# Projecting q and k of the last four head groups beside sliding-window attention, with x loaded a second time

## The chip, the cores and the metric

The kernel runs on one core of one Trainium2 chip. The metric is the device time of the whole launch in microseconds (us); lower is better. The engines named below are PE (matrix multiply; PEld is its weight load), DVE (vector), ACT (activation functions), POOL (general purpose) and SP, whose queue issues every DMA of this kernel.

## The reference

The reference computes windowed attention and an MLP from the same `x` and mixes the two with a gate for each row. Cut to what matters:

```python
B, S, D = 1, 2048, 512          # F = 1792, H = 32 heads of 16, window W = 256
qkv = x @ wqkv                   # split into q, k, v, each [H, S, 16]
scores = q @ k.T * 16 ** -0.5    # kept where 0 <= row - column < 256
a = softmax(scores) @ v          # heads joined again, then a = a @ wo
b = gelu(x @ w1 + b1) @ w2 + b2
g = sigmoid((x * gate_w).sum(-1, keepdims=True))
out = g * a + (1 - g) * b
```

## The kernel before

**Precision.** Every large product is made of three matmuls (`mm3`, L109 to L111): each operand is held as a rounded high part and a low rest, and high by high, high by low and low by high are added in PSUM. One such triple of 512 columns is the unit of dense work; the kernel's own planner books `MM3` = 681 ns for it.

**Tiles.** S is cut into four tiles `t` of 512 rows (`T`), each tile into four blocks of 128. D has four chunks `c`. `wqkv` gives, for each tile, eight pieces for q and k (`qk_j`, four of each) and four for v (`v_b`). A piece is four triples. The 32 heads are eight head groups of four. Pieces j = 0, 1 of q and j = 4, 5 of k hold head groups 0 to 3, and j = 2, 3, 6, 7 hold groups 4 to 7.

**Dense work.** `dense()` is a generator that yields after each triple. It goes through `qkv(t)` for four tiles, then through eight turns of the MLP (`TURNS`: half of F, tile), each of them a part u (7 tiles of `x @ w1`, with the GELU as four ACT and three DVE instructions behind each) and a part y (the product with `w2`), and at last through `final(t)`, the product with `wo` (tile name `a`).

**Attention.** It runs through 128 units `u` of 128 keys (8 groups by 16 blocks). In each there are four scores for the row maximum (`sm`, L522, reduced on DVE at L527, 12 units ahead), four scores transposed (`st`, L567, then exp on ACT at L589) and, behind every fourth unit, a run of small matmuls with v (`pv`, L611). Loads for it go four units and more ahead: `kd`, `qd`, `ks`, `qs`, `vbuf`.

**Order.** All five engines run in the order in which the program was written out. A planner interleaves the two streams by a clock `now` of its own: `fill(ns)` takes that much dense work from the generator, `after(ns, f)` writes f out so many ns later, `need(key)` writes out what is due until key is there. Dense work alone fills the first `START` = 105 us of the planner's clock. From there each attention unit is followed by `STEP0` = 2750 ns (before u = 0) or `STEP` = 2330 ns of dense work, spread over the unit's four scores: behind each pair of them, or behind each single one while an MLP u part is running. With these numbers the MLP's last turn ends when the attention does.

**q and k.** A piece is moved out of PSUM by ACT (high, L323) and DVE (low, L326) into a buffer of tag `h` (7 buffers) and stored to DRAM by two DMAs of 512 and 256 KB (`SQ`, `SK`); the attention loads are made from there. Weights come in as `raw` tiles, are split by ACT (L179) and by DVE or POOL (L183) into tag `w` (14 buffers); the list `later` holds those of the MLP and of `wo`. After `LAND` = 7500 ns from a load the planner writes out the ACT copy, which waits for the landing and holds up what stands behind it on ACT.

**x.** The transposed, split x of tile t is a buffer of 4 chunks by 512 KB. It is stored to DRAM (`XT`) and loaded again for each MLP turn (`mx`, tag `xt`, one buffer).

Of the kernel before, what the change touches and what calls it, by code (L numbers as in the profile page):

```python
# [18 lines left out]
T = 512  # L19
# [13 lines left out]
def gated_mix(ctx: ExitStack, tc: tile.TileContext, x, wqkv, wo, w1, b1, w2, b2, gate_w, out):  # L33
# [74 lines left out]
    def mm3(p, lh, ll, rh, rl, first, last):  # L108
        nc.tensor.matmul(p, lh, rh, start=first, stop=False)  # L109
        nc.tensor.matmul(p, lh, rl, start=False, stop=False)  # L110
        nc.tensor.matmul(p, ll, rh, start=False, stop=last)  # L111
# [19 lines left out]
    def need(*keys):  # L131
        for key in keys:
            while key not in done:
                step_todo()
# [154 lines left out]
    def gate_z(t, b):  # L289
# [2 lines left out]
        nb = t * NB + b  # L292
        nc.vector.tensor_tensor_reduce(junk, xr, gwb, 1.0, 0.0, ALU.mult, ALU.add, z[:, nb:nb + 1])

    def qkv_qk(t, j):

        xt = xts[t]
        w = wt["qk", j]
        p = ps.tile([128, T], F32, tag="d", bufs=2, name=f"qk{t}_{j}")
        for c in range(NC):  # L300
            mm3(p, w[:, 0, c], w[:, 1, c], xt[:, c, 0], xt[:, c, 1], c == 0, c == NC - 1)
            yield MM3
        qk_out(t, j, p)

# [59 lines left out]
    def warm(n):  # L364

        p = ps.tile([128, T], F32, tag="d", bufs=2, name=f"warm{now[0]}")
        for _ in range(n):
            nc.tensor.matmul(p[:, 0:320], idle[:, 0:128], idle, start=True, stop=True)
            tick(134)

    def qkv(t):
        last = t == NT - 1
        qk = [("qk", j) for i in range(NC) for j in (i, i + NC)]
        vs = [("v", b) for b in range(NB)]
        pieces = qk[:4] + vs + qk[4:] if last else qk + vs
        if t == 0:
            keys = qk + [("v", c) for c in range(NC)]
            load_xr(0, (0, 1))
            load_raw(keys[0], True)
            load_xr(0, (2, 3))  # L380
            for key in keys[1:]:
# [12 lines left out]
            split_now(keys[1], lambda o, i: nc.scalar.activation(o, i, AF.Copy), nc.vector)  # L394
            qkv_x(0, 3)
            parts = [(0, 0), (0, 1), (1, 0)]
            yield qk_half(p[1], j1, 0, parts)
            split(keys[2], nc.gpsimd)
            yield qk_half(p[0], j0, 1, parts)
            qk_out(0, j0, p[0])  # L400
            yield qk_half(p[1], j1, 1, parts)
            qk_out(0, j1, p[1])
        need(*[("x", t, b) for b in range(NB)])
        for n, (kind, j) in enumerate(pieces):
            if not last and XAT <= n < XAT + NC:
                nc.sync.dma_start(XT[t][n - XAT], f32(xts[t][:, n - XAT]))
            if kind == "qk":
                need(("w", (kind, j)))
            else:
                need(*[("w", ("v", c)) for c in range(NC)])  # L410
            if t == 0 and n == 10:
                nc.sync.dma_start(b1c, b1.rearrange("(f p) -> p f", p=128))
            if t == 0 and n < 2:
                pass
            elif kind == "qk":
                yield from qkv_qk(t, j)
            else:
                yield from qkv_v(t, j)
            if t == 1 and n % 3 == 2:
                clear_k(n // 3)  # L420
# [4 lines left out]
            if t == 2 and n in (8, 9):  # L425
                load_ks(0, n - 8)
            if t == 0:
                for i in ([3], [4], [5], [6], [7], [8], [9, 10], [11])[n] if n < 8 else []:
# [11 lines left out]
            xat = (5, 7, 8, 9) if t == 0 else (4, 6, 8, 10)  # L440
            if not last and n in xat:
                qkv_x(t + 1, xat.index(n))
            if not last and n == xat[-1] + 1:
                gate(t + 1)


    vts, Ms, pts = {}, {}, {}

# [224 lines left out]

    w1k = w1.rearrange("(c p) f -> p c f", p=128)

    def load_x(t, name):
        xt = sb.tile([128, NC, 2, T], F32R, tag="xt", bufs=1, name=f"{name}{t}")

        def part(c):
            nc.sync.dma_start(f32(xt[:, c]), XT[t][c])  # L680
            if c == NC - 1:
                done.add(name)
        for c in range(NC):
            after(MXAT * c, part, c)
        xts[t] = xt

    def load_o(t, cs=range(NC)):
# [82 lines left out]
    def mlp(n):  # L770
# [9 lines left out]
        for i in range(HF):  # L780
# [266 lines left out]
```

## Time and profile before

| | |
|---|---|
| timed runs | 749.82, 750.41, 750.96 us; median 750.41 |
| span of the profiled execution | 747.5 us |
| instructions in it | 17960 |
| PE busy | 732.3 us (98%) |
| DVE, ACT, POOL busy | 519.5, 421.8, 372.5 us |
| granted PE clock | 1.000 over the whole span |
| bytes moved by DMA | 172.12 MB, mean 230 GB/s |

The span reaches from the first to the last instruction of one profiled execution. That execution's time as a launch isn't listed by itself; the timed runs lie 2.3 to 3.5 us above the span. A matmul's end is modelled: one of 512 columns reads as 0.39 us long while the next starts 0.23 us after it, so the first 0.16 us of any wait of PE don't show as idle. In the profile's windows each stretch gives busy time and instruction counts for each engine, then the granted clock, the busy share of the DMA engines and the rate.

### The profile page before, as it was taken

To read this page: it belongs to the slowest core of one execution; us is meant where nothing else is said; L and a number is where in the kernel's file an instruction comes from. 1 tells how busy PE (TensorE), PEld (TensorE's weight loads), DVE (VectorE), ACT (ScalarE), POOL (GpSimd) and SP (SyncE) were. 2 spreads that over 40 slices of the span, in tenths; PEclk is the share of its full clock that TensorE was granted. 3 is DMA by queue.
4 is the path that set the end of the run, shared out by engine and by line. 5 is a ranking of instruction groups with operands and counts; after the bars stand their busy time and mean duration, and the time that the engine had idled before them with its cause. 6 is when DMAs were issued, how large, how long until landed. Compare 5 with 4: busy or idle time off the path is not lost.

```text
span 747.5 us, 17960 instructions
## 1 busy us (share of the span) xinstructions
PE 732.3 (98%) x6129; PEld 604.7 (81%) x6129; DVE 519.5 (69%) x1567; ACT 421.8 (56%) x972; POOL 372.5 (50%) x846
## 2 busy tenths in 40 slices
PE   8999999998999999999999999999999999999998
PEld 7888888876788888888887877888888888867786
DVE  4632425799768867886898689768867986784552
ACT  4434532358437835764695478437745853794550
POOL 4200000339756865876587668747765875630000
PEclk9999999999999999999999999999999999999999
DMA  9979898898995687799566889996799789558673
GB/s 318 336 243 408 288 391 282 254 311 194 263 258 132 173 238 205 178 220 265 155 169 156 237 209 232 257 231 154 179 262 238 185 204 287 138 179 230 205 235 113
DMA packets 179259, 172.12 MB, mean 230 GB/s; under 512 B 56672, under 2 KB 122976, under 8 KB 179168
## 3 DMA queue, kind: packets, MB, share of 16 engines
q1 hardware_dynamic: 179168, 170.97, 82.0%
q8 instruction: 49, 0.80, 0.5%
q14 instruction: 42, 0.34, 0.2%
HBM read 108.53 MB, written 62.39 MB: 229 GB/s over the span
## 4 chain that ended last, share of the span: by engine, by line
PE 85%; DVE 4%; DMA 3%; ACT 3%; issue 3%; POOL 1%; SPq 0%; DVEq 0%; ACTq 0%; POOLq 0%
PE sm L522 9%; PE st L567 8%; PE pv_sm L611 7%; PE y L109 7%; PE y L110 6%; PE y L111 6%; PE u L109 5%; PE u L110 5%; PE u L111 5%; PE qk L109 4%; PE qk L111 4%; PE qk L110 4%; PE a L109 2%; PE v L109 2%; PE v L111 2%
## 5 line engine op out<-in xcount | busy, mean ns | idle before, releaser
L527 DVE CUSTOM_DVE_ANT_0 jm<-sm,mask 128x320 bf16<-128x320 f32 (+4 forms) x512 | 237.9, 465 | 95.4 <-PE sm L522 61.0
L583 POOL TENSOR_SCALAR_AFFINE_SELECT pt<-pt 64x256 f32<-64x256 f32 (+1 forms) x538 | 227.6, 443 | 109.4 <-ACT pt L589 99.1
L589 ACT ACTIVATE pt<-st 128x320 f32<-128x320 f32 (+4 forms) x512 | 199.6, 424 | 139.0 <-PE st L567 135.4
L522 PE MATMUL sm<-kd,qd 96*128 96x320 f32 (+4 forms) x512 | 153.9, 312 | 6.9 <-DVE M L527 6.1
L567 PE MATMUL st<-qs,ks 128*128 128x320 f32 (+4 forms) x512 | 154.0, 309 | 1.9 <-ACT pt L589 1.9
L549 POOL CAST qs<-tt 4x256 fp32r<-4x256 f32 x256 | 124.2, 485 | 53.2 <-DVE tt L542 42.6
L522 PEld LDWEIGHTS sm<-kd,qd 96*128 96x128 f32 x512 | 96.4, 188 | 33.6 <-DVE M L527 14.2
L567 PEld LDWEIGHTS st<-qs,ks 128*128 128x128 f32 x512 | 97.1, 190 | 18.9 <-ACT pt L589 3.3
L109 PE MATMUL y<-w,h 128*128 128x512 f32 x224 | 88.6, 395 | 0.0
L110 PE MATMUL y<-w,h 128*128 128x512 f32 x224 | 87.9, 392 | 0.0
L111 PE MATMUL y<-w,h 128*128 128x512 f32 x224 | 87.9, 392 | 0.0
L109 PE MATMUL u<-mx,w 128*128 128x512 f32 x196 | 80.0, 408 | 0.0
L110 PE MATMUL u<-mx,w 128*128 128x512 f32 x196 | 77.3, 395 | 0.0
L111 PE MATMUL u<-mx,w 128*128 128x512 f32 x196 | 77.0, 393 | 0.0
L611 PE MATMUL pv_sm<-pt,vbuf 64*32 64x320 f32 (+4 forms) x1408 | 73.6, 346 | 0.2
L611 PE MATMUL pv_st<-pt,vbuf 64*32 64x320 f32 (+4 forms) x1408 | 73.3, 346 | 0.0
L611 PEld LDWEIGHTS pv_sm<-pt,vbuf 64*32 64x32 f32 x1408 | 50.2, 106 | 20.1 <-issue 2.4
L326 DVE TENSOR_TENSOR qke<-qk,qke 128x512 fp32r<-128x512 f32 x32 | 22.0, 688 | 45.9 <-ACT qke L323 38.5
L323 ACT ACTIVATE qke<-qk 128x512 fp32r<-128x512 f32 x32 | 19.1, 597 | 55.4 <-PE qk L111 32.9
L111 PEld LDWEIGHTS y<-w,h 128*128 128x128 f32 x224 | 42.1, 188 | 9.9
L339 POOL MEMSET vx<- 128x32 f32 x16 | 2.4, 156 | 89.4 <-DMA SQ<-qke 42.4
L611 PEld LDWEIGHTS pv_st<-pt,vbuf 64*32 64x32 f32 x1408 | 46.1, 106 | 0.0
(148 smaller groups left out, 1332.6 us busy)
## 6 DMA issues: line engine op xcount, KB each, us to landing
kd<-SK SPq DMA_DIRECT2D x32, 384.0 KB
qs<-SQ SPq DMA_DIRECT2D x64, 192.0 KB
mx<-XT SPq DMA_DIRECT2D x24, 512.0 KB
SQ<-qke SPq DMA_DIRECT2D x16, 512.0 KB
SK<-qke SPq DMA_DIRECT2D x16, 512.0 KB
ND<-nd SPq DMA_DIRECT2D x32, 256.0 KB
raw_w<-in_B_w_dram SPq DMA_DIRECT2D x28, 256.0 KB
ks<-SK SPq DMA_DIRECT2D x32, 192.0 KB
```

Source lines behind the costliest of these rows:

```text
L109: nc.tensor.matmul(p, lh, rh, start=first, stop=False)
L110: nc.tensor.matmul(p, lh, rl, start=False, stop=False)
L111: nc.tensor.matmul(p, ll, rh, start=False, stop=last)
L323: nc.scalar.activation(e[:, h], p, AF.Copy)
L326: nc.vector.tensor_sub(e[:, 1 - h], p, f32(e[:, h]))
L522: nc.tensor.matmul(p[:, :w], qd[0:96, n, pr, 128 * j:128 * (j + 1)], kd[0:96, n, pr, k1 - w:k1], start=True, stop=True)
L527: nc.vector.tensor_tensor_reduce(junk[:, :w], p[:, :w], mask[:, 320 - w:320], 1.0, -3e38, ALU.add, ALU.max, M[:, 2 * (b % RB) + hb, pr:pr ...
L549: nc.gpsimd.tensor_copy(dst, src.unsqueeze(1).broadcast_to([4, 2, RB, 32]))
L567: nc.tensor.matmul(p[:, :w], ks[:, slot(g_, kb // NB), pr, at:at + 128], qs[:, pr, k0:k0 + w], start=True, stop=True)
L583: nc.gpsimd.affine_select(out=v, in_=v, pattern=[[0, v.shape[1]], [1 - 2 * e, 64]], compare_op=ALU.is_ge, fill=0.0, base=-e, channel_multi ...
L589: nc.scalar.activation(pt[:, hf, pr, :w], p[:, :w], AF.Exp, scale=SCALE)
L611: nc.tensor.matmul(pv[r // 64][32 * i:32 * i + 32, q - c * T:e - c * T], vts[g_, b // NB][r:r + 64, v:v + 32], rhs(r), start=start, stop=s ...
```

## The change

q and k of the last four head groups leave `qkv(t)`, which now makes eight pieces for each tile (`EARLY`: q and k of groups 0 to 3, and v). The other 16 pieces are made by a new generator `qkv_rest`, which stands between the last `qkv` and the first MLP turn, in the order of tiles 3, 0, 1, 2. Tile 3 is still in place; the x of tiles 0, 1 and 2 is loaded again from `XT` (12 loads of 512 KB more than before): tiles 0 and 2 go, one after the other, into four of the seven `h` buffers, and tile 1 goes into the `xt` buffer, where the first MLP turn then finds it. The stores of `XT` of tile 3, which stood behind the first u part, stand in the first four pieces of the rest. Attention begins after 70 us of the planner's clock in place of 105, so that the last pieces are made beside it. A unit now gets 2400 ns of dense work while q and k are projected, 2950 in u parts and 2370 in y parts, in place of 2330 throughout. Weights loaded after 60 us of the planner's clock (before: 152 us) use the two `raw` buffers, with the low part always on DVE: five of the first 14 MLP weights were split on POOL before, none now.

```diff
+    QK = [("qk", j) for i in range(NC) for j in (i, i + NC)]
+    EARLY = QK[:NC] + [("v", b) for b in range(NB)]
...
-        qk = [("qk", j) for i in range(NC) for j in (i, i + NC)]
-        vs = [("v", b) for b in range(NB)]
-        pieces = qk[:4] + vs + qk[4:] if last else qk + vs
...
-        for n, (kind, j) in enumerate(pieces):
+        for n, (kind, j) in enumerate(EARLY):
...
-            if last and n not in (6, 7):
-                load(later.pop(0))
-            if last and n == len(pieces) - 1:
-                for _ in range(4):
-                    load(later.pop(0))
+            if t in (1, 2) and n >= NC:
+                (load_raw(QK[n], True) if t == 1 else split(QK[n], nc.gpsimd))
...
+    def load_again(t):
+        if t == REST4[2]:
+            load_x(t, f"again{t}", XAGAIN)
+            return
+        xts[t] = [sb.tile([128, 2, T], F32R, tag="h", bufs=7, name=f"xa{t}_{c}") for c in range(NC)]
+
+        def part(c):
+            nc.sync.dma_start(f32(xts[t][c]), XT[t][c])
+            if c == NC - 1:
+                done.add(f"again{t}")
+        for c in range(NC):
+            after(XAGAIN * c, part, c)
+
+    def qkv_rest():
+        done.add(f"again{NT - 1}")
+        for m, t in enumerate(REST4):
+            need(f"again{t}")
+            if m + 1 < NT:
+                load_again(REST4[m + 1])
+            for n, (kind, j) in enumerate(QK[NC:]):
+                if m == 0:
+                    nc.sync.dma_start(XT[t][n], f32(xts[t][:, n]))
+                yield from piece(t, kind, j)
+                if m * NC + n in LOADS:
+                    load(later.pop(0))
+        for _ in range(4):
+            load(later.pop(0))
...
-    TURNS = [(0, 3), (0, 0), (0, 1), (0, 2), (1, 2), (1, 0), (1, 1), (1, 3)]
+    TURNS = [(0, 1), (0, 0), (0, 3), (0, 2), (1, 2), (1, 0), (1, 1), (1, 3)]
...
-        if n == 0:
-            for c in range(NC):
-                nc.sync.dma_start(XT[t][c], f32(xt[:, c]))
...
         for t in range(NT):
             yield from qkv(t)
+        yield from qkv_rest()
...
-        step = STEP if u >= 0 else STEP0
+        step = STEPS[stage[0]] if u >= 0 else STEP0
...
-RAWS = 152000.0
+RAWS = 60000.0
...
-START = 105000.0
+START = 70000.0
...
-STEP = 2330.0
+STEPS = {"qk": 2400.0, "u": 2950.0, "y": 2370.0}
+REST4 = (3, 0, 1, 2)
+LOADS = {0, 2, 4, 6, 7, 9, 10, 12, 13, 15}
+XAGAIN = 2500.0
```

The two orders below show it. First SP's queue, before the change, where the last q and k pieces of tile 3 are stored (`SQ3`, `SK3`; the digit behind a name is the tile, `raw_w1` and `raw_w2` are MLP weights, `kd` and `qd` are attention loads):

```order
L330 DMA SQ3_82<-qke3_2_1530 128x2x512
L331 DMA SQ3_82<-qke3_2_1530 128x512
L171 DMA raw_w16_1535<-in_B_w2_dram 128x512
L330 DMA SK3_86<-qke3_6_1567 128x2x512
L331 DMA SK3_86<-qke3_6_1567 128x512
L491 DMA kd_76<-SK2_85 96x2x256
L491 DMA kd_76<-SK3_86 96x2x512
```

And SP's queue now at the store of the same piece of tile 3, the first of the rest (`XT3` is the store of x, `xa0` the second load of tile 0):

```order
L468 DMA XT3_94<-xt3_814 128x1024
L171 DMA raw_w10_1320<-in_B_w1_dram 128x4x128
L454 DMA xa0_2_1273<-XT0_91 128x1024
L334 DMA SQ3_82<-qke3_2_1314 128x2x512
L335 DMA SQ3_82<-qke3_2_1314 128x512
L468 DMA XT3_94<-xt3_814 128x1024
L519 DMA kd_76<-SK2_85 96x2x256
L519 DMA kd_76<-SK3_86 96x2x512
L511 DMA qd_75<-SQ3_82 48x8x128
L506 DMA qd_75<-SQ3_82 48x7x128
L508 DMA qd_75<-SQ3_82 48x2x64
L454 DMA xa0_3_1274<-XT0_91 128x1024
```

Between two stores of a piece there now stand loads and stores of x besides what stood there before. From the first matmul of the rest to the last, SP's rows add up to 31.6 MB; PE has 192 dense matmuls, 60 full and 8 short `sm`, 46 `st` and two `pv` runs there.

On PE, where a u part runs beside attention, before (`u0_2` is an MLP piece, `sm1_12` and `st1_0` are attention units):

```order
L110 MATMUL u0_2_2810<-mx00_2149,w1_2_1418 128x512
L111 MATMUL u0_2_2810<-mx00_2149,w1_2_1418 128x512
L522 MATMUL sm1_11_2_2820<-kd_76,qd_75 128x320
L567 MATMUL st0_15_3_2824<-qs_73,ks_74 128x64
L522 MATMUL sm1_12_1_2827<-kd_76,qd_75 128x320
L567 MATMUL st1_0_0_2833<-qs_73,ks_74 128x320
L109 MATMUL u0_2_2810<-mx00_2149,w1_2_1418 128x512
```

And the same place in the u part of that turn now:

```order
L111 MATMUL u0_1_3427<-mx00_2843,w1_1_1499 128x512
L550 MATMUL sm2_7_2_3468<-kd_76,qd_75 128x320
L595 MATMUL st1_11_3_3471<-qs_73,ks_74 128x320
L109 MATMUL u0_1_3427<-mx00_2843,w1_1_1499 128x512
L110 MATMUL u0_1_3427<-mx00_2843,w1_1_1499 128x512
L111 MATMUL u0_1_3427<-mx00_2843,w1_1_1499 128x512
L550 MATMUL sm2_8_1_3483<-kd_76,qd_75 128x320
L595 MATMUL st1_12_0_3488<-qs_73,ks_74 128x320
```

Before, a score here and there had no triple behind it; with the longer step each of them has one, and a u part, whose 84 matmuls are the same, holds 25 `sm` and 25 `st` where most held 32 or 33 of each. The y parts keep their 33. The numbers of matmuls of each kind over the whole program are the same as before.

More of the change, by code (lines that the diff above doesn't have):

```diff
@@ L369, in warm, with piece @@
             tick(134)
+    QK = [("qk", j) for i in range(NC) for j in (i, i + NC)]
+    EARLY = QK[:NC] + [("v", b) for b in range(NB)]
+    def piece(t, kind, j):
+        if kind == "qk":
+            need(("w", (kind, j)))
+            yield from qkv_qk(t, j)
+        else:
+            need(*[("w", ("v", c)) for c in range(NC)])
+            yield from qkv_v(t, j)
     def qkv(t):
         last = t == NT - 1
-        qk = [("qk", j) for i in range(NC) for j in (i, i + NC)]
-        vs = [("v", b) for b in range(NB)]
-        pieces = qk[:4] + vs + qk[4:] if last else qk + vs
         if t == 0:
-            keys = qk + [("v", c) for c in range(NC)]
+            keys = QK[:NC] + [("v", c) for c in range(NC)] + QK[NC:]
             load_xr(0, (0, 1))
@@ L380, in qkv @@
             load_xr(0, (2, 3))
-            for key in keys[1:]:
+            for key in keys[1:2 * NC]:
                 load_raw(key, True)
@@ L403, in qkv @@
         need(*[("x", t, b) for b in range(NB)])
-        for n, (kind, j) in enumerate(pieces):
+        xat = (3, 5, 6, 7) if t == 0 else (2, 4, 5, 6)
+        for n, (kind, j) in enumerate(EARLY):
             if not last and XAT <= n < XAT + NC:
                 nc.sync.dma_start(XT[t][n - XAT], f32(xts[t][:, n - XAT]))
[L407 to L411, printed above, removed]
-                nc.sync.dma_start(b1c, b1.rearrange("(f p) -> p f", p=128))
[L413 to L420, printed above, removed]
+            if t == 0 and n == 5:
+                nc.sync.dma_start(b1c, b1.rearrange("(f p) -> p f", p=128))
+            if t > 0 or n > 1:
+                yield from piece(t, kind, j)
+            if t == 1 and n % 2 == 1:
+                clear_k(n // 2)
             if t == 2 and n < 4:
@@ L424, in qkv @@
                 load_kd(0, n - 1)
-            if t == 2 and n in (8, 9):
-                load_ks(0, n - 8)
+            if t == 2 and n in (5, 6):
+                load_ks(0, n - 5)
             if t == 0:
-                for i in ([3], [4], [5], [6], [7], [8], [9, 10], [11])[n] if n < 8 else []:
+                for i in ([3], [4, 5], [6], [7])[n] if n < 4 else []:
                     split(keys[i], nc.vector if i % 2 else nc.gpsimd)
@@ L434, in qkv @@
                 load_xr(t + 1)
-            if last and n not in (6, 7):
-                load(later.pop(0))
-            if last and n == len(pieces) - 1:
-                for _ in range(4):
-                    load(later.pop(0))
-            xat = (5, 7, 8, 9) if t == 0 else (4, 6, 8, 10)
+            if t in (1, 2) and n >= NC:
+                (load_raw(QK[n], True) if t == 1 else split(QK[n], nc.gpsimd))
             if not last and n in xat:
                 qkv_x(t + 1, xat.index(n))
-            if not last and n == xat[-1] + 1:
+            if not last and n == len(EARLY) - 1:
                 gate(t + 1)
+    def load_again(t):
[18 more added lines that the diff above has]
+                    nc.sync.dma_start(XT[t][n], f32(xts[t][:, n]))
+                yield from piece(t, kind, j)
+                if m * NC + n in LOADS:
+                    load(later.pop(0))
+        for _ in range(4):
+            load(later.pop(0))
     vts, Ms, pts = {}, {}, {}
@@ L674, in gated_mix, with load_x @@
     w1k = w1.rearrange("(c p) f -> p c f", p=128)
-    def load_x(t, name):
+    def load_x(t, name, apart=None):
         xt = sb.tile([128, NC, 2, T], F32R, tag="xt", bufs=1, name=f"{name}{t}")
@@ L683, in load_x @@
         for c in range(NC):
-            after(MXAT * c, part, c)
+            after((apart or MXAT) * c, part, c)
         xts[t] = xt
```

5 lines of the change are left out of this document (4 added, 1 removed).

## The prediction

> **What bounds the kernel now.** I read the head of the page first, then who kept PE waiting, then the windows of each stage, and the DMA rates last.
>
> ```profile
> span 747.5 us, 17960 instructions
> ...
> PE 732.3 (98%) x6129; PEld 604.7 (81%) x6129; DVE 519.5 (69%) x1567; ACT 421.8 (56%) x972; POOL 372.5 (50%) x846
> ...
> PE sm L522 <- DVE M L527: 6.1, 11, 1.0
> PE st L567 <- ACT pt L589: 1.9, 3, 1.2
> ```
>
> PE is busy for 98% of the span, so what the change can win is bounded by PE's gaps, and the waits name them: PE waits for DVE, which still reduces an earlier score, or for ACT. No row has PE waiting for a DMA. The windows say where. Each row is one u or y part, in the order of the program (the columns are the busy time of each engine with its count, the clock, the DMA share and GB/s):
>
> ```profile
> 150.40:184.70 34.30, 31.45 (x209) 24.33 (x209) 31.59 (x94) 25.36 (x52) 21.69 (x38) 1.00 0.98 244
> 184.70:220.20 35.50, 34.54 (x345) 28.72 (x344) 24.66 (x86) 17.06 (x42) 24.41 (x62) 1.00 0.97 267
> 220.20:254.00 33.80, 33.74 (x320) 28.66 (x319) 28.50 (x92) 25.27 (x58) 23.87 (x51) 1.00 0.60 142
> 254.00:288.30 34.30, 34.30 (x344) 28.73 (x343) 23.79 (x84) 16.16 (x40) 23.23 (x60) 1.00 0.87 244
> ...
> 356.70:391.10 34.40, 33.79 (x319) 28.04 (x318) 30.33 (x93) 27.27 (x62) 23.00 (x48) 1.00 0.64 165
> 391.10:426.80 35.70, 34.52 (x342) 28.40 (x341) 27.14 (x91) 18.19 (x44) 25.23 (x61) 1.00 0.73 184
> 426.80:463.30 36.50, 34.83 (x320) 27.94 (x319) 31.96 (x97) 28.32 (x64) 24.30 (x48) 1.00 0.90 219
> 463.30:498.80 35.50, 34.79 (x343) 28.49 (x343) 26.00 (x90) 16.83 (x42) 23.71 (x60) 1.00 1.03 266
> ...
> 566.90:600.30 33.40, 33.40 (x319) 28.17 (x318) 28.44 (x93) 25.77 (x58) 23.93 (x51) 1.00 0.76 194
> ...
> 667.00:697.50 30.50, 29.30 (x310) 23.05 (x310) 17.50 (x38) 19.03 (x49) 0.00 (x0) 1.00 0.73 213
> ```
>
> A u part without gaps takes 33.4 to 33.8 us (220.2, 566.9), with DVE busy for 28.5 of them. The u parts at 150.4, 356.7 and 426.8, which also split weights, have DVE at 30.3 to 32.0 us and PE short of the window by 0.6 to 2.9 us. So DVE is what bounds a u part, and PE bounds a y part (DVE 24 of 34).
>
> **What the stalls cost.** The rhythm of PE without a stall, from a u part:
>
> ```profile
> 238.64 0.40 PE L109 MATMUL u<-mx,w 128*128 128x512 f32 x1
> 238.88 0.39 PE L110 MATMUL u<-mx,w 128*128 128x512 f32 x1
> 239.10 0.39 PE L111 MATMUL u<-mx,w 128*128 128x512 f32 x1
> 239.34 0.31 PE L522 MATMUL sm<-kd,qd 96*128 96x320 f32 x1
> 239.49 0.31 PE L567 MATMUL st<-qs,ks 128*128 128x320 f32 x1
> 239.64 0.39 PE L109 MATMUL u<-mx,w 128*128 128x512 f32 x1
> ```
>
> From start to start that is 0.70 us for a triple and 0.15 us for each score. Stage by stage against its like: the u parts at 356.7 and 426.8 are 0.8 and 2.9 us over 33.6. The first u part has 111 PE instructions less than the next one, which are 14 scores (2.1 us) and a `pv` run (2.3 us, row below), so 29.2 us of work stand in its 34.3 us: 5.1 us of stall. The y parts at 184.7, 391.1 and 463.3 are over 34.4 by 1.1, 1.3 and 1.1 us. Another 2 us lie in the parts not shown and in the last y part, whose window falls 1.2 us short. Together 14.3 us; the idle time in these rows is less, since the first 0.16 us of each wait lie under the modelled end of the matmul before.
>
> **The change, part by part.** *PE's work* is the same: equal counts of each kind of matmul, so moving 16 pieces costs PE nothing by itself. Removed with the shorter start is nothing either; the 35 us of planner's time that attention begins earlier come back as longer steps. Everything hangs on how the stalls change.
>
> *Longer steps in u parts* (2950 for 2330 ns): a u part has 8 scores of each kind less. What DVE pays for a score:
>
> ```profile
> L527 DVE CUSTOM_DVE_ANT_0 jm<-sm,mask 128x320 bf16<-128x320 f32 (+4 forms) x512 | 237.9, 465 | 95.4 <-PE sm L522 61.0
> ...
> L611 PE MATMUL pv_sm<-pt,vbuf 64*32 64x320 f32 (+4 forms) x1408 | 73.6, 346 | 0.2
> ...
> L527 DVE DVE_READ_ACCUMULATOR2_ANT M<- 128x1 f32 x512 | 41.7, 81 | 0.0
> ...
> L183 DVE TENSOR_TENSOR w<-raw_w,w 128x512 fp32r<-128x512 f32 x23 | 17.4, 758 | 0.0
> ```
>
> The two L527 rows are 0.546 us together, so DVE is relieved of 8 x 0.546 = 4.4 us, and PE of 16 x 0.15 = 2.4 us and half a `pv` run (73.6 us over 32 runs is 2.3 us each, one for four units, that is for 16 scores of a kind), 3.5 us together. Where DVE had 28.5 us in 33.6 it has 24.1 in 30.1, 80% in place of 85%; in the part at 426.8 it had 32.0 against 33.6 of PE's work, 95%, and will have 27.6 in 30.1, 92%. The first u part had 31.6 against 29.2; with 25 scores of each kind and a full `pv` load it has about 28.3 against 30.4. So the pressure that made the stalls is lower everywhere, but not gone where weights are split. I take 10 us of the 14.3 as won. The ends are 4 us (only the first u part's stall goes) and all 14.3. The y parts gain 0.04 us of dense work for each unit, nothing that a row can price.
>
> *x loaded again, and q and k beside attention.* SP issues 31.6 MB between the first and the last matmul of the rest. What each of them is:
>
> ```profile
> mx<-XT SPq DMA_DIRECT2D x24, 512.0 KB
> SQ<-qke SPq DMA_DIRECT2D x16, 512.0 KB
> ...
> raw_w<-in_B_w_dram SPq DMA_DIRECT2D x28, 256.0 KB
> ...
> SQ<-qke SPq DMA_DIRECT2D x16, 256.0 KB
> ```
>
> 16 pieces of 768 KB are 12.6 MB, 12 loads of x 6.3 MB, the store of tile 3's x 2.1 MB, ten weights 2.6 MB, and 8 MB are attention's loads and the bias. PE's work there is 192 x 0.233 + 106 x 0.15 + 8 x 0.08 + 2 x 2.3 = 65.8 us. That asks for 480 GB/s. What the queue has delivered:
>
> ```profile
> 55.00:75.00 20.00, 20.00 (x98) 16.56 (x97) 5.04 (x8) 8.36 (x23) 0.63 (x4) 1.00 1.04 407
> ...
> 145.00:165.00 20.00, 19.33 (x93) 16.09 (x92) 17.72 (x58) 9.16 (x18) 7.43 (x12) 1.00 1.05 325
> ```
>
> The best 20 us ran at 407 GB/s with the engines full (share 1.04), in the stage that stores pieces and x; with attention's smaller loads among them 325 was reached, also with a full share. So the transfers take 31.6 / 0.407 = 77.6 us at best, 11.8 more than PE's work. Not all of this reaches PE. How late the queue may run unseen:
>
> ```profile
> L326 DVE TENSOR_TENSOR qke<-qk,qke x32: 650/691/692, 12.9 to 152.1; 128x512 fp32r<-128x512 f32 x32
> ...
> L330 SPq DMA_DIRECT2D SK<-qke x16: 371/888/1204, 15.1 to 157.5; - x16
> ...
> 154.05 0.38 SPq L330 DMA_DIRECT2D SQ<-qke  x1
> 154.48 0.47 SPq L331 DMA_DIRECT2D SQ<-qke  x1
> 154.99 0.93 SPq L758 DMA_DIRECT2D ya<-in_B_b_dram  x1
> ```
>
> The last piece's low part was started on DVE at 152.1 and its store issued at 157.5, with SP issuing one DMA after another, 0.4 to 0.9 us each: some 4 us late, and PE waited for no DMA. The loads of x are begun four pieces ahead (16 us of PE at 65.8 / 16 a piece), which allows more; but a weight's copy stands on ACT 7.5 us of planner's time behind its load, and ACT waits for it in order, with the exps behind. I take 6 us as what stays unseen, which leaves 6 us on PE. The ends: 0, if four pieces' lead covers all of the 11.8; and 31.6 / 0.325 - 65.8 - 4 = 27 us, if the whole stage runs at the lower rate and only the seen 4 us are free. I stay near the lower end since some three quarters of the bytes are stores and loads like those of the 407 row.
>
> The Trainium skill, "DMA: Bandwidth & Descriptors", section "Where 436 GB/s comes from", sets about 358 GB/s for a core's share of HBM below the 435 of the ports, and says that the HBM side binds. By it the transfers would take 88 us, and the sum would come out slower than before. The trace held 407 over 20 us on this one core, so I don't take it as a ceiling here.
>
> *Small things.* Five low parts move from POOL to DVE (0.76 us each by L183's row above, 3.8 us) into a stage with no GELU, where DVE pays 2.2 us of scores for each 4.2 us unit: hidden. Each new issue costs SP about 0.5 us, 6 us for the 12 loads; it counts in the queue's lateness above. The store of tile 3's x leaves the first y part, which was 1.1 us over: included in the 10. Losing four `h` buffers leaves three for the pieces: a piece comes every 4.1 us, so a store may take 12 us from the copy before ACT must wait. That cover goes if the queue is over 10 us late, and then exps are late next.
>
> Sum: -10 + 6 = -4 us, a span of 743.5; the median stands 2.9 above the span, and 750.4 - 4 = 746.4 us.
>
> **Rivals.** *(1) The transfers are hidden.* The lead of four pieces absorbs the 11.8 us, and 10 to 14.3 us are won: 736.1 to 740.4. For it: PE waited for no DMA even where the share was over 1.0. Against: that was at 325 to 407 GB/s, not with 480 asked for.
>
> *(2) The rest runs at DMA speed.* At 365 GB/s, midway between the two rows, 31.6 MB take 86.6 us, and with 6 us unseen PE loses 14.8: 750.4 - 10 + 14.8 = 755. Place: PE waits at the first matmul that reads a reloaded chunk, or `st` waits for ACT, which holds at a weight's copy. It decides where the rate falls under 31.6 / (65.8 + 6 + 10) = 386 GB/s. For it: the 145 us row, and that this stage has more attention loads than the 407 row. The page of the Trainium skill named above would put its price at 88.3 - 71.8 - 10, 6.5 us slower than before.
>
> *(3) The u parts stay bound.* With a longer step more GELU falls to a unit, ACT and DVE both stay near full, and only 4 us are won against 6 paid: 752.4. For it: 92% of DVE in the parts that split weights. Against: parts at 85% have no gap at all.
>
> **Chances.** Differences within 0.2% (1.5 us) can hardly be told from none here. Stalls mostly gone with part given back, 0.42, from which 0.36 end as faster and 0.06 within; transfers hidden 0.20; at DMA speed 0.22, of which 0.04 come out even; u parts still bound 0.16, of which 0.06 even. That gives faster 0.56, same 0.16, slower 0.28. The likeliest case alone spans 741 to 750; the range goes from 736, all stalls gone and nothing paid, to 758, between rival 2's price and its upper end.
>
> **What would show it.** Right: u parts of 30 to 31 us with PE's window filled; waits of `sm` for DVE well under 6.1 us; between about 105 and 180 us a DMA share over 1.0 at 380 GB/s or more, and there a few waits of PE for a reloaded chunk or for ACT, adding up to some 6 us. Rival 1: no PE idle there. Rival 2: idle of 10 us and more, SP issuing without a break. Rival 3: u parts over 32 us with `sm` waiting for DVE. The prediction fails if the rate under the mixed load is far from 390, or if splitting weights on DVE stalls the rest as it did the first u part.

## The result, and the profile after

The changed kernel takes 783.88 us (median of 4 runs, 782.04 to 786.61) against 750.12 us, a ratio of 1.0453 with a 95% interval of 1.042 to 1.0486. The forecast was 746.4 us; the time lies 26 us above the upper end of the range. The head of the page after:

```profile
span 780.9 us, 17945 instructions
...
PE 744.7 (95%) x6129; PEld 614.2 (79%) x6129; DVE 522.9 (67%) x1570; ACT 423.5 (54%) x972; POOL 356.8 (46%) x843
...
PEclk9999999798999999999999999999999999999999
...
PE 69%; DMA 15%; DVE 4%; SPq 3%; issue 2%; ACT 2%; DVEq 0%; ACTq 0%
```

PE has the same 6129 matmuls. The chain that ended last now goes through DMA for 15% of the span, and the granted clock, 1.00 throughout before, dips in two slices. The windows by stage place the loss (after first; the columns are busy time of each engine with its count, the clock, the DMA share and GB/s):

```profile
3.60:203.70 200.10, 179.02 (x981) 147.70 (x981) 101.43 (x310) 76.79 (x194) 51.97 (x138) 0.94 0.95 310
203.70:243.20 39.50, 34.53 (x329) 27.88 (x328) 28.40 (x81) 25.20 (x57) 17.62 (x39) 0.96 0.83 219
243.20:728.20 485.00, 481.09 (x4515) 399.60 (x4515) 369.88 (x1144) 302.95 (x690) 286.25 (x660) 1.00 0.77 201
...
728.20:780.90 52.70, 47.68 (x303) 37.87 (x301) 23.17 (x38) 17.27 (x31) 0.00 (x0) 0.99 0.56 181
```

And the same stages before (q, k and v; all u and y parts; the last product):

```profile
3.70:150.40 146.70, 145.75 (x707) 122.06 (x707) 68.84 (x180) 57.80 (x145) 22.38 (x56) 1.00 0.94 320
...
150.40:697.50 547.10, 537.39 (x5116) 443.44 (x5116) 427.52 (x1352) 345.53 (x798) 349.11 (x784) 1.00 0.82 210
697.50:747.50 50.00, 46.65 (x301) 37.98 (x299) 23.09 (x38) 17.16 (x29) 0.00 (x0) 1.00 0.57 191
```

The first stage now holds 58 more `sm`, 48 `st` and two `pv` runs, 20.5 us of work by the prices of the prediction (0.15 and 2.3 us). It grew by 53.4 us, so 32.9 are lost there. The u and y parts should be 20.5 us shorter, 526.6; they are 39.5 + 485.0 = 524.5. The first of them is 39.5 us for the 30.4 us of work that the prediction set, 9.1 us of stall where it had 5.1 before. So the other fifteen parts won some 6 us, the first lost 4, and 2.1 remain. The last product costs 2.7 us more. Together 32.9 - 2.1 + 2.7 = 33.5 us, the difference of the spans (33.4).

What PE waits for while the late pieces are made, and what the queue does there (the first row is the stage of the late pieces, from its first matmul to the first u part; the second reaches 16 us into that part):

```profile
115.70:203.70 88.00, 74.96 (x479) 62.02 (x478) 51.23 (x176) 32.27 (x75) 32.82 (x88) 0.88 1.04 326
...
120.00:220.00 100.00, 86.41 (x619) 71.32 (x618) 58.57 (x197) 39.44 (x89) 40.45 (x108) 0.90 1.06 329
```

```profile
124.21 7.85 DMA SQ<-qke
132.08 7.13 DMA xa<-XT
139.26 0.79 PE qk L109
...
148.16 9.29 DMA again<-XT
157.46 6.70 DMA raw_w<-in_B_w_dram
...
166.71 8.48 DMA SQ<-qke
175.21 7.55 DMA raw_w<-in_B_w_dram
```

The stage of the late pieces takes 88.0 us, 22.2 more than the 65.8 us of work that the prediction counted for it. So of the 32.9 us lost, 10.7 are lost before the late pieces begin, in the four tiles of eight pieces. The DMA engines are full for 100 us (share 1.06) at 329 GB/s, and the second fence, from the chain of waits, goes from one DMA to the next: each takes 7 to 9 us to land, with hardly any work of PE between. It is not x alone: stores of pieces and weights stand in the chain as much. Among the waits from 85 us on, PE's own show mostly as `st` for ACT (8.1 us) and `sm` for DVE (5.0 us), with one wait for a reloaded chunk of x and one of 2.3 us for an attention load (`qd`). ACT meanwhile stands at weights, and at buffers that a store still reads:

```profile
ACT w L179 <- DMA raw_w<-in_B_w_dram: 26.0, 10, 5.6
...
PE st L595 <- ACT pt L617: 8.1, 3, 3.6
...
PE qk L109 <- DMA xa<-XT: 3.6, 1, 3.6
...
ACT qke L327 <- DMA SK<-qke: 7.8, 1, 7.8
```

### The profile page after: what moved, and what is told of

Same layout as the page of the kernel before. It is cut to its first block, busy times and chain, and to the rows that moved or that the text cites. A ratio compares the mean times of both kernels' runs of the same rounds, so it can differ in the third digit from the quotient of the medians.

```text
span 780.9 us, 17945 instructions
## 1 busy us (share of the span) xinstructions
PE 744.7 (95%) x6129; PEld 614.2 (79%) x6129; DVE 522.9 (67%) x1570; ACT 423.5 (54%) x972; POOL 356.8 (46%) x843
## 4 chain that ended last, share of the span: by engine, by line
PE 69%; DMA 15%; DVE 4%; SPq 3%; issue 2%; ACT 2%; DVEq 0%; ACTq 0%
PE sm L550 8%; PE st L595 8%; PE y L109 6%; PE pv_sm L639 6%; PE y L110 6%; PE y L111 6%; PE u L109 6%; PE u L110 6%; PE u L111 6%; DMA raw_w<-in_B_w_dram 3%; DMA SQ<-qke 3%; DMA SK<-qke 2%; PE pv_st L639 2%; DMA SV<-vx 2%; DVE jm L555 1%
## 5 line engine op out<-in xcount | busy, mean ns | idle before, releaser
L611 POOL TENSOR_SCALAR_AFFINE_SELECT pt<-pt 64x256 f32<-64x256 f32 (+1 forms) x538 | 217.1, 423 | 156.5 <-ACT pt L617 146.8
L617 ACT ACTIVATE pt<-st 128x320 f32<-128x320 f32 (+4 forms) x512 | 200.0, 422 | 145.7 <-PE st L595 135.1
L550 PEld LDWEIGHTS sm<-kd,qd 96*128 96x128 f32 x512 | 97.8, 191 | 34.6 <-DVE M L555 10.7
L595 PEld LDWEIGHTS st<-qs,ks 128*128 128x128 f32 x512 | 98.3, 192 | 26.9 <-ACT pt L617 10.8
L111 PEld LDWEIGHTS y<-w,h 128*128 128x128 f32 x224 | 42.1, 188 | 9.9
L109 PEld LDWEIGHTS y<-w,h 128*128 128x128 f32 x224 | 42.4, 189 | 4.8 <-ACT sqh L753 0.6
```

Of the source, the lines that this page charges most:

```text
L550: nc.tensor.matmul(p[:, :w], qd[0:96, n, pr, 128 * j:128 * (j + 1)], kd[0:96, n, pr, k1 - w:k1], start=True, stop=True)
L595: nc.tensor.matmul(p[:, :w], ks[:, slot(g_, kb // NB), pr, at:at + 128], qs[:, pr, k0:k0 + w], start=True, stop=True)
L611: nc.gpsimd.affine_select(out=v, in_=v, pattern=[[0, v.shape[1]], [1 - 2 * e, 64]], compare_op=ALU.is_ge, fill=0.0, base=-e, channel_multi ...
L617: nc.scalar.activation(pt[:, hf, pr, :w], p[:, :w], AF.Exp, scale=SCALE)
```

## The experiments

Theory A: the stage of the late pieces runs at the speed of the DMA queue, and PE's clock adds to each wait. Theory B: the earlier start of attention, or the order, costs it. Theory C: single things are late, x or a buffer. Times are medians; the kernel before lay at 749.2 to 750.2 us beside them.

**No second load of x.**

```diff
-            nc.sync.dma_start(f32(xts[t][c]), XT[t][c])
+            nc.gpsimd.memset(f32(xts[t][c]), 0.0)
```

> The changed kernel without the twelve second loads of x: the same buffers are filled with zeros by POOL, so the last 12 of the 16 late pieces are made from zeros. 6.3 MB fewer go through SP's queue between about 95 and 190 us; every order of PE, DVE and ACT stays. Theory A (the stage from 120 to 220 us runs at the speed of the queue, 329 GB/s on the mean of its windows, and PE's clock falls after each wait): 6.3 MB at 0.329 are 19 us less to transfer, some 12 to 20 us of the 33.8 come back, 764 to 772 us, and the clock stays nearer 1.0 between 120 and 220 us. Theory B (attention begun earlier and the order of the splits cost it, not the bytes): within 3 us of 783.9. Theory C (PE waits for the reloaded x alone, the rest of the queue is in time): about the 8 us which the waits for x show, 774 to 777.

767.55 us. 16.3 us came back, the clock's mean rose from 0.982 to 0.993, and the 80 us from 120 on still ran at a share of 1.06 and 326 GB/s. The stage of the late pieces is 17.1 us shorter (70.9 for 88.0):

```profile
116.90:187.80 70.90, 67.62 (x480) 56.95 (x479) 51.82 (x176) 32.20 (x75) 43.29 (x99) 1.00 1.05 319
```

So what came back came back there. Of the forecasts only Theory A's was met; B and C as they stood do not hold. The rate is as low without these loads as with them: their price is the bytes that they add, 6.3 MB in 16 to 17 us. Another 18 us remained.

**Steps by stage alone, in the kernel before.**

```diff
-        step = STEP if u >= 0 else STEP0
+        step = STEPS[stage[0]] if u >= 0 else STEP0
...
+STEPS = {"qk": 2330.0, "u": 2650.0, "y": 2090.0}
```

> The kernel before, with only the dense time of a unit set by stage: 2330 ns while q and k are projected, 2650 in u parts, 2090 in y parts; no second pass, no second load of x, start of attention as before. If the gain of the u parts is a thing by itself, as in the prediction (10 of 14.3 us): a u part that had 32 or 33 scores of each kind now has 28 to 29, stalls go down, 741 to 747 us. If y parts, which get more scores, lose as much to DVE as u parts win: 749 to 753.

752.83 us, ratio 1.0052 (1.0033 to 1.0071). Its stages:

```profile
150.50:696.90 546.40, 538.62 (x5115) 445.19 (x5113) 424.97 (x1350) 345.96 (x795) 348.68 (x784) 0.99 0.83 210
696.90:751.50 54.60, 47.80 (x302) 37.92 (x301) 23.76 (x40) 17.79 (x32) 0.00 (x0) 1.00 0.52 176
```

All u and y parts together won 0.7 us only: the u parts have fewer scores (the one at 356.8 us is 32.0 us for 34.4), the y parts more. The last product lost 4.6 us.

**Attention's start undone, second pass kept.**

```diff
-START = 70000.0
+START = 105000.0
...
-STEPS = {"qk": 2400.0, "u": 2950.0, "y": 2370.0}
+STEPS = {"qk": 2330.0, "u": 2650.0, "y": 2090.0}
```

> The changed kernel with attention begun after 105 us of the planner's clock again, in place of 70, and steps of 2330, 2650 and 2090 ns, so that both streams still end together: the second pass and the second load of x stay, but about 35 us of attention are taken out of the stage that reloads x. Theory A (rate of the queue): the 23.6 MB of pieces, x and weights stay in the rest, 23.6 / 0.407 = 58 us against 44.7 us of dense PE work for 192 matmuls, so waits of 10 to 15 us stay, 755 to 768 us. Theory B (the early start itself costs it): 738 to 748, u parts as in the changed kernel and no loss in the rest.

779.66 us, more than either theory said. Against the run before, which has the same start and steps and no second pass, the second pass costs 26.8 us. It needs hardly any attention beside it to do so; in the first 20 us below PE ran six `sm`:

```profile
120.00:140.00 20.00, 13.30 (x54) 9.62 (x53) 5.40 (x16) 3.21 (x6) 0.00 (x0) 0.96 1.05 355
...
162.00:167.00 5.00, 4.54 (x21) 3.31 (x19) 2.70 (x10) 0.60 (x1) 0.00 (x0) 1.00 1.16 278
...
120.00:180.00 60.00, 47.54 (x198) 36.49 (x197) 31.58 (x104) 12.68 (x22) 6.94 (x16) 0.94 1.06 364
```

This run also shows which loads go with a low rate. From 140.0 to 155.9 us SP issued stores of pieces, four loads of x and three of weights, and the queue moved 403 GB/s:

```profile
DMA packets 3594, 6.41 MB, mean 403 GB/s; under 512 B 244, under 2 KB 1389, under 8 KB 3593
...
xa<-XT SPq DMA_DIRECT2D x4, 512.0 KB
...
raw_w<-in_B_w_dram SPq DMA_DIRECT2D x3, 256.0 KB
```

From 155.9 to 160.2 us it issued five of attention's (`kd` twice, then `qd` three times); from 162 to 167 us, at a share of 1.16, the rate was 278 GB/s.

**One step for all stages in the changed kernel** (2600 ns).

> The changed kernel with one step of 2600 ns in every stage: only the setting by stage is undone. Theory A: the rest is bound by the transfers, so its time does not follow the step of q and k (2600 for 2400 puts 8% fewer attention loads into it, 1 to 2 us better), while u parts get 28 to 29 scores of each kind for 25 and get back 1 to 3 us of stall each: 784 to 800. If the setting by stage is what cost the time: under 775.

782.78 us, the same as the changed kernel within 0.2% and a little under what was expected. Its u and y parts take 527.0 us (524.5 with steps by stage), its last product 50.1 (52.7). The fifteen parts behind the first, with as many matmuls of each kind, take 488.6 us for 485.0, so the setting by stage won 3.6 us there; the first u part and the last product gave it back.

**The late start without the second loads** (both edits above).

> The kernel with attention begun at 105 us again and steps of 2330, 2650 and 2090 ns (779.7 us), now also without the twelve second loads of x: POOL fills the same buffers with zeros. What is left of the change is the order of the pieces. Theory A (queue): the 6.3 MB taken out are 17 us at the 364 GB/s measured there between 120 and 180 us, so 17 to 22 us of the 26.8 us that the second pass costs come back: 758 to 763; the remaining 6 to 8 stand in the first 100 us, where PE waits for x of the next tile. If the order of the pieces itself stalls PE: over 768.

763.61 us: 16.1 us of the 26.8 are the second loads, as in the first run. The other 10.8 us are all that is left of the change: the order of the pieces above all, but also the splits of the weights on DVE, the buffers that x takes and the order of the turns. Against the kernel with steps by stage alone, by the spans, the first stage is 12.2 us longer (159.1 for 146.9), the u and y parts 4.9 shorter (541.5 for 546.4) and the last product 3.0 longer (57.6 for 54.6). In the first 40 us PE was busy for 37.83 us before, and here:

```profile
0.00:40.00 40.00, 34.62 (x169) 27.19 (x170) 16.77 (x33) 15.01 (x37) 10.26 (x34) 0.96 0.76 260
```

With eight pieces to a tile in place of twelve, the next tile's x is needed sooner, and PE waits for it.

**x in other buffers**, so that pieces have seven `h` buffers again (late start).

```diff
-        xts[t] = [sb.tile([128, 2, T], F32R, tag="h", bufs=7, name=f"xa{t}_{c}") for c in range(NC)]
+        xts[t] = [sb.tile([128, 1280], F32R, tag="pt", bufs=PTS, name=f"xa{t}_{c}")[:, 0:2 * T]
+                  .rearrange("p (s t) -> p s t", s=2) for c in range(NC)]
```

> The kernel with attention begun at 105 us again (779.7 us), with the second x of tiles 0 and 2 put into the buffers of exp (tag pt, not yet in use there) in place of four of the seven h buffers. All bytes and all orders stay; pieces of q and k have seven buffers again in place of three. Theory A (the queue's rate): the bytes of the stage stay, so 772 to 780, since PE must wait for the transfers in one way or another. Rival C (the three buffers: ACT waits for a store, DVE for ACT, the score maximum for DVE, PE for the maximum): PE waits in the rest go away, 758 to 766.

779.42 us for 779.66, with the same 364 GB/s from 120 to 180 us. Waits for ACT and DVE only turned into waits for x. The three buffers are not the cause.

**Three waits put into PE's row** of the kernel before.

```diff
+        nc.tensor.matmul(p, idle[:, 0:128], idle, start=True, stop=True)
+        for _ in range(n):
+            nc.vector.tensor_copy(idle, p)
+        nc.tensor.matmul(p, idle[:, 0:128], idle, start=True, stop=True)
```

> The kernel before, with three waits put into PE's row while q and k of tile 2 are projected: behind pieces 0, 4 and 8 a small matmul of zeros waits for 4, 8 and 16 copies in a row on DVE (about 0.4 to 0.5 us each, so waits of about 2, 4 and 8 us). It measures what a wait costs PE by itself: if only the wait is lost, 14 us in all, 764; if the granted clock falls behind the longer waits as it did in the changed kernel (0.66 to 0.83 in windows of 10 us), matmuls of 512 columns start 0.43 us apart for some microseconds and the loss is 18 to 24 us, 768 to 774, with the short wait free of it.

770.6 us (one run), 21.3 us more for waits of 2.5, 4.6 and 8.8 us from start to start, 15.8 in all. The second and the third, as PE's row shows them (start, length):

```profile
93.97 0.31 PE L374 MATMUL sp<-idle 128*128 128x320 bf16 x1
98.54 0.31 PE L377 MATMUL sp<-idle 128*128 128x320 bf16 x1 [4.26 <-DVE idle L376]
...
100.09 0.63 PE L109 MATMUL qk<-qs,qk 128*128 128x512 f32 x1
...
120.92 0.45 PE L377 MATMUL sp<-idle 128*128 128x320 bf16 x1 [8.46 <-DVE idle L376]
...
126.72 0.44 PE L111 MATMUL v<-v,qs 128*128 128x512 f32 x1
```

After the short wait matmuls came 0.23 us apart at once. After 4.6 us they came 0.43 us apart from 99.7 to 102.7, after 8.8 us until 126.7: some 1.5 and 3 us more. In the changed kernel the 4.22 us from `sm` at 135.04 to `qk` at 139.26 are of this kind, and the first wait for x halves the clock after only 2.75 us (the last row is a window, with the granted clock of 0.50 behind the counts):

```profile
19.67 0.39 PE L111 MATMUL qk<-ks,qk 128*128 128x512 f32 x1
22.42 1.11 PE L262 MATMUL xp<-ident,xr 128*128 128x128 f32 x4 [2.37 <-DMA xr<-in_A_x_dram]
...
24.19 0.63 PE L111 MATMUL v<-v,ks 128*128 128x512 f32 x1
...
135.04 0.63 PE L550 MATMUL sm<-kd,qd 96*128 96x320 f32 x1 [2.23 <-DVE M L555]
139.26 0.79 PE L109 MATMUL qk<-xa,qk 128*128 128x512 f32 x1 [3.59 <-DMA xa<-XT]
...
135.10:145.30 10.20, 6.61 (x16) 5.10 (x17) 3.78 (x12) 1.23 (x2) 0.00 (x0) 0.50 1.06 359
```

The Trainium skill, "TensorE: Matmul & The Clock Gate", section "What's actually happening", says that PE falls to half its clock after an idle window of about 3.4 us and needs about as long a busy one to come back. The traces agree in part: in the changed kernel the clock stood at half for 3.4 us from 22.4, for 10.2 us from 135.1 and for 6.8 us from 182.9, which are one, three and two such windows. But no length of wait marks the border here: 2.75 us sufficed, and so did 2.31 us in the run without the second loads and with the late start (127.93 to 130.24), while the wait of 2.47 us in this run cost nothing.

**Steps of 2500 and 2160 ns in the kernel before.**

> The kernel before with dense time of 2500 ns for a unit in u parts and 2160 in y parts (2330 while q and k are projected); the sum over a u and a y part is that of before, so attention ends where it did. If the 4.5 us that the last stage lost with 2650 and 2090 came from attention ending later, the last stage is 50 us again and half of the u parts' stalls are won: 744 to 748. If y parts lose what u parts win: 749 to 752.

748.94 us, ratio 0.9995 (0.9983 to 1.0007): no difference. The last product is 47.7 us, but only because its `pv` run has moved into the last y part, and the u and y parts take 547.6 us for 547.1.

**Second loads in packets of 512 bytes** (changed kernel; each load in two DMAs that take every other 128 columns).

> The changed kernel with each second load of x split into two DMAs that take every other run of 128 columns, so that the same 6.3 MB come in packets of 512 bytes in place of 4 KB; the rest is unchanged. Theory A in its sharper form (the queue's rate falls with the size of packets: 407 GB/s where they average 2.1 KB, 329 where 1.26 KB): 6.3 MB at about 280 GB/s, an estimate below the 329, take 22 us in place of 15, so 6 to 12 us more with what the clock adds, 790 to 796 us, and under 310 GB/s between 120 and 220 us. If bytes alone count: 783 to 786.

788.91 us, 5.0 more: less than expected. From 120 to 220 us, this kernel first and the changed one behind:

```profile
DMA packets 36379, 32.24 MB, mean 322 GB/s; under 512 B 5510, under 2 KB 27092, under 8 KB 36369
```

```profile
DMA packets 26245, 32.93 MB, mean 329 GB/s; under 512 B 5458, under 2 KB 15258, under 8 KB 26235
```

39% more packets lowered the rate by 2%. Packets of 512 bytes in place of 4 KB do not explain 329 against 407. Packets under 512 bytes, of which attention's loads bring most (5458 in these 100 us), were not varied.

**x of the next tile earlier**, and its transposes later, in the changed kernel, and in the kernel with the late start and without second loads.

```diff
-        xat = (3, 5, 6, 7) if t == 0 else (2, 4, 5, 6)
+        xat = (4, 5, 6, 7)
...
-                    after(4000, load_xr, 1)
+                    after(1500, load_xr, 1)
```

> The changed kernel with x of the next tile loaded 2.5 us earlier for tile 1, and its transposes behind pieces 4 to 7 of every tile in place of 3, 5, 6, 7 and 2, 4, 5, 6. PE's waits for x in the first 100 us (3.7 us, and the half clock behind the first of them, 6 to 7 us in all against before) should go: if they reach the end, 776 to 779 us. If the queue's backlog sets when the rest goes on anyway, an earlier arrival there is given back: 781 to 784.

> The kernel with attention begun at 105 us, steps of 2330, 2650 and 2090 ns and zeros in place of the second loads of x (763.6 us), now also with the transposes of x behind pieces 4 to 7 and the load of tile 1's x 2.5 us earlier. If the waits for x in the first 100 us are what is left of the second pass's price beside the reload (763.6 against 752.8 without the second pass): 756 to 759. If they are not: 762 to 764.

787.67 us for 783.88, and 763.70 for 763.61. The waits for x went away; in their place PE waits for the copies of the transposed x on ACT (1.1 us at each tile) and, at 90 us, 5.5 us for an attention load. The second kernel's first stage is 1.4 us shorter, and its time is the same. So the waits for x alone do not set the 10.8 us; other waits took their place, and which of them count is not settled by these two edits.

**Half of the weights split on POOL, with 2500 and 2160 ns,** in the kernel before.

```diff
-            after(LAND, split, key, nc.vector, True)
+            after(LAND, split, key, nc.gpsimd if key[1] % 2 else nc.vector, True)
```

> The kernel before with two edits against the u parts' stalls, and no second pass: 2500 ns for a unit in u parts and 2160 in y parts, and every other MLP weight's low part split on POOL (1.33 us there) in place of DVE (0.76 us). DVE is relieved of about ten splits, 7.6 us in all, in the parts where it stands at 92 to 95 per cent; POOL pays 13 us where it has 30 per cent idle. If DVE's queue is what makes PE wait: 742 to 747. If POOL's exps wait behind the splits instead: 749 to 753.

751.33 us, ratio 1.0025 (1.0011 to 1.0039): 0.25% slower. No version here beats the kernel before.

**Loads put among the stores of the kernel before**, beside tile 1's pieces: five of attention's kind, then four of x's kind.

```diff
+            if t == 1 and 2 <= n < 7:
+                load_kd(0, 0)
```

```diff
+            if t == 1 and 2 <= n < 6:
+                nc.sync.dma_start(f32(kd.rearrange("p a b c -> p (a b c)")[:, 0:2 * T]), XT[0][n - 2].rearrange("p s t -> p (s t)"))
```

> The kernel before with five more attention loads (kd of head group 0, 384 KB each into 96 partitions, nothing reads them) issued beside pieces 3 to 7 of tile 1, where the queue ran at 407 GB/s and a packet of 2 KB took 84 ns. It asks why the same 2 KB packets took 97 ns on the mean in the stage of the changed kernel. If loads of attention's kind slow the queue: under 370 GB/s between 55 and 75 us with the share at 1.0, and a mean over 92 ns for packets of 2 KB. If not: 395 GB/s or more, 84 to 87 ns, and only the 2 MB are paid (5 us of queue, hidden, 749 to 752).

> The control to the one before: at the same place four loads of stored x (512 KB each into 128 partitions in packets of 4 KB, nothing reads them), 2.1 MB. If loads of any kind among the stores slow the queue, as much as kd does: under 370 GB/s between 55 and 75 us. If only attention's kind does: 400 GB/s or more here.

758.94 and 756.5 us (one run each; the kernel before 748.94 beside them). The same 20 us, with kd, then with x:

```profile
55.00:75.00 20.00, 20.00 (x98) 16.57 (x97) 5.01 (x8) 8.40 (x23) 0.63 (x4) 1.00 0.96 345
```

```profile
55.00:75.00 20.00, 20.00 (x95) 16.49 (x94) 5.34 (x8) 8.24 (x20) 0.63 (x4) 1.00 0.98 357
```

Where the queue moved 407 GB/s at a share of 1.04 it moves 345 and 357 at 0.96 and 0.98, with more to do than before. What stood in the 407 row were stores alone, by the list of DMAs issued there:

```profile
XT<-qd SPq DMA_DIRECT2D x4, 512.0 KB
SQ<-qke SPq DMA_DIRECT2D x3, 512.0 KB
SK<-qke SPq DMA_DIRECT2D x3, 512.0 KB
SQ<-qke SPq DMA_DIRECT2D x3, 256.0 KB
SK<-qke SPq DMA_DIRECT2D x3, 256.0 KB
SV<-vx SPq DMA_DIRECT2D x2, 136.0 KB
SV<-vx SPq DMA_DIRECT2D x3, 68.0 KB
```

That is 1.25 and 1.0 MB less in 20 us. But these two runs do not price a load by itself. Each added load writes the same place of `kd` as the one before it, and SP stood still until that one had landed, 10.0 us in four waits with `kd` and 9.1 us in three with x; in the kernel before, its longest wait in that stretch was 0.6 us:

```profile
SPq L493 <- DMA kd<-SK: 10.0, 4, 2.9
```

```profile
SPq L420 <- DMA kd<-XT: 9.1, 3, 3.6
```

In these pauses the engines ran dry in part, as the shares of 0.96 and 0.98 show. The lateness reached PE: some 45 us later the first load of `qd` came late, a new wait in both kernels, and the clock was slow behind it (0.79 from 118 to 128 us with `kd`):

```profile
PE sm L524 <- DMA qd<-SQ: 5.8, 1, 5.8
```

```profile
PE sm L524 <- DMA qd<-SQ: 4.2, 1, 4.2
```

**Loads from another queue** (changed kernel): the second loads of x from ACT's queue, from POOL's, and x and the MLP weights from ACT's.

```diff
-            nc.sync.dma_start(f32(xts[t][c]), XT[t][c])
+            nc.scalar.dma_start(f32(xts[t][c]), XT[t][c])
```

> The changed kernel with the twelve second loads of x issued from ACT's queue in place of SP's; nothing else is moved. In the two runs before, each load put among the stores on SP's queue cost about 0.6 us of transfer at 407 GB/s (1.25 MB fewer moved for five loads, 1.0 MB for four), on top of its own bytes. Theory D (a load between stores on one queue makes the engines pause): with a queue of their own these loads overlap the stores, 12 x 0.6 = 7 us of queue come back, the rate between 120 and 220 us goes over 340 GB/s, 772 to 778 us. Theory A in its first form (the engines are full whatever the queue): 782 to 787. A third way: the loads wait on ACT for buffers and hold up exps behind them: over 790.

> The same twelve loads issued from POOL's queue. Theory D: 772 to 778 as from ACT, and less where ACT was held up. Theory A: 782 to 787.

> The second loads of x and all 28 loads of MLP weights issued from ACT's queue, so that SP's queue has only stores and attention's loads in the stage from 120 to 220 us. [...] Theory A: 782 to 787.

784.15, 793.89 and 780.92 us. The third is 3 us better than the changed kernel, and from 120 to 220 us the rate is 324, 295 and 321 GB/s for 329, none over the 340 that Theory D asked for. Theory D fell: with a queue of their own the loads do not raise the rate. The times alone would not have shown it, since in the first of these runs ACT stood for 17.6 us until stores of tile 3's x had landed. Nor is the 0.6 us for each load, on which Theory D was built, a price of the load: SP's waits stand in it. The Trainium skill, "DMA: Bandwidth & Descriptors", section "Issuing engines are not separate DMA queues", says that DMAs from all engines run on the same 16 DMA engines and only save issue time; the three runs agree. On POOL the loads came later still (PE waits 12.9 us for `xa`).

## Why the prediction was wrong

*The gain in the u parts: right in its direction, wrong in its size.* `sm` waits for DVE for 6.7 us in all of the program, 5.0 of them beside the late pieces, so what is left for the u and y parts is well under the 6.1 us before; three u parts take 31.7, 32.9 and 30.5 us. But 10 us were taken and 2.1 came: the fifteen parts behind the first won some 6 of their 9.2 us of stall, and the first one, whose 5.1 us were to go, stalls for 9.1. It stands behind the same queue, which is full until 220 us.

*The DMA term, 6 us with ends 0 and 27: wrong, and it is the step that failed.* The stage of the late pieces lost 22.2 us. The choice that was mis-sized is the rate. 407 GB/s was taken because three quarters of the bytes are "like those of the 407 row"; the stage ran at 329, next to the other row's 325, with attention's loads in both. So 31.6 MB take 96 us for 65.8 us of PE's work, 30 us. Of these 8 did not show in the stage itself, so the 6 us unseen were of the right size, though some of them came out in the first u part. The loads of x are not what lowers the rate: it is 326 without them, and 403 where they stand among stores and weights with none of attention's loads. That attention's loads set it fits these three stretches, but no run took them out, so it is argued and not shown.

*Left out.* The four tiles of eight pieces lost 10.7 us before the late pieces began; moving pieces was said to cost PE nothing. In the first 40 us PE is 34.29 us busy for 37.83. The clock: some waits of 2.3 us and more cost 1.5 to 3 us beside themselves. The last product, 2.7 us.

*Small things: in part.* The three buffers did make ACT wait for stores (7.8 and 3.6 us), as said for a late queue, but giving seven back changed nothing.

*The rivals.* Rival 2, at DMA speed, was the way it went, at 329 in place of the 365 GB/s taken for it; its own formula gives 750.4 - 10 + (96 - 71.8) = 764.6, and the rest is the gain that did not come and what was left out. The 358 GB/s that the prediction cites from the Trainium skill is no ceiling here, since the kernel before held 407 in a stretch of stores, and the changed kernel's 329 lies below it. What would show the forecast wrong was named: a rate far from 390. Rival 3's gain, 4 us, was nearer to the 2.1 than the forecast's 10.

By the prediction's terms, in spans: gain 2.1 for 10, DMA 22.2 for 6, the tiles before 10.7 for nothing, the last product 2.7 for nothing: -2.1 + 22.2 + 10.7 + 2.7 = 33.5 us.

The account by runs, in medians: steps by stage +3.6, order of the pieces and what goes with it +10.8, second loads +16.1, earlier start with its steps +4.2, together 34.7 from 749.2 to 783.9.

What stays open: why the engines move less while attention's loads are among the transfers, and which waits make up the 10.8 us of the order and the 10.7 us before the late pieces.

## What to carry to other kernels

Take the rate for a moved transfer from a stretch that has the same kinds of transfer in it, small loads above all; here the full engines moved 407 GB/s in one stretch and 325 in another. Where a stage asks for more than that rate, covering the latency of its loads doesn't help; and a DMA share of 0.94 over the 147 us of the stage before already says that there is little room for 6 MB more. Where PE may wait for more than some 2 us, reckon with the slow clock behind the wait. When a load is added as a probe, give it a place of its own, or the wait for that place is measured with it.

## What was not expected of the hardware

A DMA share over 1.0 does not tell the rate: 407 GB/s at 1.04, 329 at 1.06, 278 at 1.16. Loads of x and of weights among stores moved at 403 GB/s, like stores alone. Splitting 6.3 MB of loads from 4 KB into 512-byte packets cost only 5 us. The clock halved after waits of 2.31, 2.75, 4.6 and 8.8 us and not after one of 2.47; in the changed kernel it stood at half for 3.4, 6.8 or 10.2 us.
